# A fused adaLN, state-space convolution and feed-forward kernel: the handover from the convolution's inverse transform to the feed-forward stage rebuilt

## The chip, the cores and the metric

The kernel runs on one core of a Trainium2 chip. A core has TensorE (PE, matrix products into PSUM), VectorE (DVE), ScalarE (ACT), GpSimd (POOL) and SyncE (SP, which issues most of the DMAs here). The metric is the device time of one launch in microseconds. The profile adds the trace of one execution.

## What is computed

The reference, cut to what matters (`_layernorm` has no weights; the sizes are L = 2048 rows, D = 512, N = 128, F = 1792):

```python
def _A_ref(u, ...):                    # a long convolution along L, one kernel for each of D channels
    P = jnp.exp(logdA[:, :, None] * l[None, None, :])
    K = jnp.einsum("dn,dnl,dn->dl", Cc, P, dB).real
    ...                                # y = irfft(rfft(u) * rfft(K)), zero padded to 2 L
    return y + u * Dskip[None, None, :]

def _B_ref(x, w1, b1, w2, b2):
    h = jnp.einsum("bsd,df->bsf", x, w1) + b1
    r = jnp.where(h > zero, h, zero)
    out = jnp.einsum("bsf,fd->bsd", r * r, w2) + b2
    return out

mod = (_silu(c) @ w_mod).reshape(c.shape[0], 6, 1, -1)
sa, ca, ga, sb, cb, gb = ...
h = _layernorm(x) * (1 + ca) + sa
x = x + ga * _A_ref(h, ...)
h = _layernorm(x) * (1 + cb) + sb
x = x + gb * _B_ref(h, ...)
```

## The kernel before

**Stages.** The first 285 us or so normalize the input, make the convolution's kernel for 64 channels at a time (`kgen_*`, eight chunks c = 0 to 7), transform input and kernel in two steps of matmuls (`stage1`, `stage2`), multiply the spectra on VectorE (`product_pieces`, lines 818 to 821) and take the first step of the inverse transform (lines 822 to 838): for each of four groups g of 16 channels, 16 matmuls of 128 columns (real and imaginary part of 64 positions j) go into one PSUM bank, and VectorE copies them (line 834) into `big0` and `big1`, which hold all positions of all chunks. The last chunk, 7, is the last thing of this stage.

**Handover.** `inverse(n)` (line 972) makes four row blocks s = 4n to 4n + 3 of 128 rows. For each s it takes 32 small fp32 matmuls (line 980; 32 by 32 weights `i2c`, 128 moving columns) over four positions of all chunks. Each fp32 matmul leaves two records of a weight load and a matmul in the profile, so one s is 64 records. The sums stand in four PSUM banks: `accs` (two double banks, `tg`) for even n, `tb` (the three `ps` banks and `kg`) for odd n. For n = 0 VectorE adds the input rows (line 989); for the others ScalarE copies (991) and POOL adds (994). `statistics(s)` (998) makes mean and variance on VectorE and a root on ScalarE. `prepare(s)` (1005) normalizes, transposes on TensorE (1021) into a bank of `tb`, and applies the second modulation, scale `cbc` and shift `sbc`, for each quarter q (1024 on VectorE, 1028 on ScalarE); the result h goes to SBUF, is rounded to the matmul's type (1032, `hh`) and the rest is kept apart (1034, `hl`).

**Feed-forward.** Four blocks k of 512 rows, NF = 14 slices t of 128 of F each, i = 14 k + t from 0 to 55. `ffn1(i)` (1076) is 12 matmuls of 512 columns into one bank of `tb` in turn (`tail_bank`): weights high and low against `hh` (1084, 1085), high against `hl` (1087). ScalarE makes relu (1090) and its rounded square (1091), VectorE the exact square (1092) and the rest (1093). `ffn2(i)` (1096) is 12 matmuls into `accs` (1104 to 1106), two steps behind ffn1 (LAG = 2). The rows of the blocks k + 1 are prepared while block k runs.

**What sets the order.** Each engine takes its instructions in a fixed order that `keep_order` (153) writes at build time: a list planner that places groups of instructions by their dependences (`region`, 172, whole banks for PSUM), by durations from `weight` (107) and by the longest path to the end. PE instructions that are in `in_turn` keep their order among themselves.

**Queues.** SyncE issues, in this order around the handover, the input rows (`xt`), the constants `i2c`, the slices of w2 through two staging buffers `wsts` (1043), and the rest of the rows (996). `w2_split` (1039) rounds each slice on ScalarE (929) and subtracts on POOL (930).

Of the kernel before, what the change touches and what calls it, by code (L numbers as in the profile page):

```python
# [11 lines left out]
F32 = mybir.dt.float32  # L12
# [27 lines left out]
HEAD = 4  # L40
ON_DVE = {}
# [65 lines left out]
def weight(ins):  # L107
# [3 lines left out]
    if "DMA" in type(ins).__name__:  # L111
# [10 lines left out]
            if cols == 32 and ins.ins[1].ap[0][1] == 32:  # L122
                return 42, 42 + 130
# [29 lines left out]
def keep_order(tc, traced, slots, in_turn, whole, urgent, behind):  # L153
# [18 lines left out]
    def region(a):  # L172
# [85 lines left out]
    for _ in groups:  # L258
# [7 lines left out]
        if e == "PE":  # L266
# [3 lines left out]
            cost /= level(now)  # L270
# [35 lines left out]
def tile_adaln_ssm_ffn(  # L306
# [61 lines left out]
    tiny = ctile("tiny", [P, 1])  # L368
    rsq = ctile("rsq", [P, 4])
# [80 lines left out]
    pick, second = ctile("pick", [P, 128], FR), ctile("second", [P, 1])  # L450
# [362 lines left out]
    def product_pieces(c):  # L813
        xu, sw, xk = xus[c], sws[c], xks[c]
        yr, yu = spectrum(), spectrum()
        for g in range(4):
# [5 lines left out]
            yield  # L822
        for g in range(4):
            ps = bank("ps", PS)
            for i in range(4):
                for h, y in ((0, yu), (1, yr)):
                    for m in range(2):
                        nc.tensor.matmul(  # L828
                            ps[64 * m : 64 * m + 64, 128 * i : 128 * i + 128],
                            pairs(y)[:, g, i // 2, 64 * m : 64 * m + 64, i % 2],  # L830
                            e1_sb[:, h], start=(h == 0), stop=(h == 1))
            copy = nc.vector.tensor_copy
            for r in range(2):
                copy(z4[r][c][:, :, 4 * g : 4 * g + 4], ps.rearrange("p (d r j) -> p j d r", d=4, r=2)[..., r])  # L834
# [137 lines left out]
    def inverse(n):  # L972
        banks = [t.rearrange("p (i c d) -> p i c d", i=4, c=NC) for t in (accs if n % 2 == 0 else tb)]
        for i in range(4):
            for r in range(2):
                for q in range(4):
                    qs = slice(32 * q, 32 * q + 32)
                    for g in range(4):
                        j = 4 * (4 * n + i) + g
# [3 lines left out]
                        whole[m.ins.name] = f"inverse {n} {i}"  # L983
        if n < 2:
            in_turn.update(whole)
        for q in range(4):
            y = x2[:, 4 * n : 4 * n + 4, q]
            if n == 0:
                nc.vector.tensor_add(y, cd4[:, :, q], banks[q])
            else:  # L990
                nc.scalar.copy(y, banks[q])  # L991
        for s in range(4 * n, 4 * n + 4):
            if n > 0:
# [11 lines left out]
    def prepare(s):  # L1005
        hh, hl = hbuf[s // 4 % 2]
        xn, h32 = (cs_[s], cs_[s]) if s < 4 else cs_[0:2]
        h32 = h32.rearrange("p (q x) -> p q x", q=4)
        if s < 4:
            nc.vector.scalar_tensor_tensor(  # L1010
                mv[:, s, 1:2], mv[:, s, 0:1], -1.0, rstd2[:, s : s + 1], op0=ALU.mult, op1=ALU.mult)
# [10 lines left out]
        for q in range(4):  # L1022
            if s < 4 and q > 0:
                nc.vector.tensor_scalar(
                    h32[:, q, :], tp[:, 128 * q : 128 * q + 128], cbc[:, q : q + 1], sbc[:, q : q + 1],
                    op0=ALU.mult, op1=ALU.add)
            else:
                nc.scalar.activation(
                    h32[:, q, :], tp[:, 128 * q : 128 * q + 128], AF.Identity,
                    bias=sbc[:, q : q + 1], scale=cbc[:, q : q + 1])  # L1030
# [3 lines left out]
        eng.tensor_sub(hl[:, :, 128 * (s % 4) : 128 * (s % 4) + 128], h32, ho.bitcast(F32))  # L1034
# [13 lines left out]
    inverse(0)  # L1048
    inverse(1)
    for s in range(4):  # L1050
        statistics(s)
        prepare(s)
    for i in range(2):
        w2_split(held(kp, f"k0{i}", f"w2{i}", [P, 3072], FR), 3)
    inverse(2)
    inverse(3)
# [11 lines left out]
    r2s = [late_fr[:, 1024:2048], rw[:, 6144:7168], rw[:, 7168:8192]]  # L1068
# [108 lines left out]
```

## Time and profile before

| | us |
|---|---|
| median of 3 runs | 655.47 |
| lowest, highest | 650.13, 662.59 |
| the profiled execution's own time | 654.19 |
| its span | 652.1 |
| TensorE granted clock, mean | 0.976 |

How to read it: a row of the timeline has the start in us, the time covered, the engine, the line, the operation, what is written and read (tiles without their numbers), the shape, how many instructions are merged, and in brackets the idle time of the engine just before and what ended it; "issue" means that the profile shows nothing that the engine waited for. PEld is the weight load. A row of the stages has the length, then for each of PE, PEld, DVE, ACT, POOL the busy time and the number of instructions, then the granted clock of TensorE (1.00 is full), the DMA share and GB/s.

### The profile page before, as it was taken

Reading aid. Unit: us, or ns where it says so; the run is one execution under the profiler, and the core shown is the slowest. Engines: PE = TensorE matmul, PEld = TensorE weight load, DVE = VectorE, ACT = ScalarE, POOL = GpSimd, SP = SyncE. Lnnn points to the kernel's source line nnn. Section 1 sums busy time; section 2 is a strip of 40 time slices with the busy share of each in tenths; the row PEclk is TensorE's granted clock in tenths of the full one; section 3 lists DMA queues with packets and bytes.
Section 4 is the critical chain, followed back from the end, with each engine's and each line's share of the span. In section 5 each row is a group of like instructions: output and inputs, shape, how many; then the busy total and the mean of one; then the engine's idle time right before and its main releaser. Section 6 shows DMA issues by size and latency. Waiting matters only on the chain.

```text
span 652.1 us, 20850 instructions
## 1 busy us (share of the span) xinstructions
PE 594.2 (91%) x9322; PEld 509.1 (78%) x9322; DVE 379.2 (58%) x646; ACT 347.7 (53%) x648; POOL 303.0 (46%) x251
## 2 busy tenths in 40 slices
PE   2389997999999999897769999999999999999995
PEld 2267886999899899885658888888888888888884
DVE  5797778899699789454596532533325332252223
ACT  4957999898997768433745532244322433222220
POOL 5489699999999996078976200011000100000000
PEclk9979999999999999997879999999999999999998
DMA  8932014032022405572141000100001000010001
GB/s 321 376 132 66 4 36 96 8 68 55 17 68 60 124 4 149 137 271 68 55 150 59 2 0 1 64 1 0 2 1 64 1 1 1 0 65 1 0 1 64
DMA packets 21705, 42.30 MB, mean 65 GB/s; under 512 B 3696, under 2 KB 9200, under 8 KB 20336
## 3 DMA queue, kind: packets, MB, share of 16 engines
q1 hardware_dynamic: 21184, 40.84, 20.3%
q8 instruction: 73, 1.20, 0.8%
q10 hardware_dynamic: 432, 0.14, 0.1%
q14 instruction: 16, 0.13, 0.1%
HBM read 28.39 MB, written 4.19 MB: 50 GB/s over the span
## 4 chain that ended last, share of the span: by engine, by line
PE 77%; ACT 6%; DVE 5%; POOL 4%; issue 4%; DMA 3%; SPq 0%; DVEq 0%; POOLq 0%; ACTq 0%
PE tg L1104 8%; PE tg L1105 8%; PE tg L1106 8%; PE ps L671 7%; PE ps L681 7%; PE ps L828 7%; PE ps L1085 6%; PE ps L1084 6%; PE ps L1087 6%; PE kg L809 4%; PE ps L634 3%; PE kg L1085 2%; PE kg L1084 2%; PE kg L1087 2%; ACT tables L756 1%
## 5 line engine op out<-in xcount | busy, mean ns | idle before, releaser
L1092 DVE TENSOR_TENSOR xy<-xy 128x512 f32<-128x512 f32 x56 | 45.8, 818 | 163.1 <-ACT rw L1091 106.4
L1090 ACT ACTIVATE xy<-ps,b1c 128x512 f32<-128x512 f32 x42 | 28.9, 689 | 134.5 <-PE ps L1087 134.5
L1017 POOL TENSOR_TENSOR big<-big,lo 128x512 f32<-128x512 f32 x12 | 16.0, 1332 | 158.5 <-DVE xy L1014 158.5
L681 PE MATMUL ps<-xy,t_sb 128*64 128x64 f32 x2048 | 66.7, 223 | 5.6 <-issue 3.3
L681 PEld LDWEIGHTS ps<-xy,t_sb 128*64 128x64 f32 x2048 | 63.5, 138 | 7.9 <-issue 3.6
L828 PE MATMUL ps<-e_sb,xy 128*64 128x128 f32 x1024 | 62.0, 274 | 2.8 <-issue 2.3
L828 PEld LDWEIGHTS ps<-e_sb,xy 128*64 128x64 f32 x1024 | 56.6, 138 | 4.7 <-issue 3.2
L673 ACT COPY xy<-ps 128x512 f32<-128x512 f32 x64 | 37.1, 591 | 15.3 <-PE ps L671 14.9
L789 POOL TENSOR_TENSOR rtl<-tables 128x1024 f32<-128x1024 f32 x22 | 43.4, 1971 | 0.2
L819 DVE TENSOR_TENSOR xy<-ps,xy 128x512 f32<-128x512 f32 x64 | 39.8, 680 | 2.0 <-PE ps L681 1.6
L1084 PE MATMUL ps<-h0h,w1h 128*128 128x512 f32 x88 | 35.3, 401 | 0.5 <-ACT big L991 0.5
L834 DVE COPY big<-ps 128x256 f32<-128x256 f32 x64 | 24.1, 417 | 19.8 <-PE ps L828 19.8
L765 POOL TENSOR_TENSOR llph<-lo,big 128x1024 int32<-128x1024 int32 x16 | 34.7, 2169 | 0.7 <-ACT tg L777 0.7
L765 POOL TENSOR_TENSOR rtl<-lo,big 128x1024 int32<-128x1024 int32 x16 | 34.3, 2142 | 1.5 <-ACT tg L777 1.0
L671 PE MATMUL ps<-d_sb,ksb 128*64 128x128 f32 x512 | 33.9, 275 | 1.1 <-DVE xy L819 0.8
L1090 ACT ACTIVATE xy<-kg,b1c 128x512 f32<-128x512 f32 x14 | 9.7, 690 | 47.1 <-PE kg L1087 42.8
L671 PE MATMUL ps<-d_sb,big 128*64 128x128 f32 x512 | 31.6, 274 | 0.8 <-ACT big L637 0.7
L1084 PE MATMUL ps<-h,w1h 128*128 128x512 f32 x80 | 31.6, 395 | 0.0
L1093 DVE TENSOR_TENSOR rw<-xy,rw 128x512 fp32r<-128x512 f32 x37 | 28.6, 774 | 2.9
L671 PEld LDWEIGHTS ps<-d_sb,ksb 128*64 128x64 f32 x512 | 28.1, 137 | 2.5 <-DVE xy L819 1.0
L671 PEld LDWEIGHTS ps<-d_sb,big 128*64 128x64 f32 x512 | 28.4, 137 | 1.6 <-ACT big L637 1.0
L800 DVE TENSOR_TENSOR rtl<-rtl,tg 128x1024 f32<-128x1024 f32 x22 | 26.7, 1213 | 2.4 <-POOL rtl L789 2.4
(260 smaller groups left out, 1604.0 us busy)
## 6 DMA issues: line engine op xcount, KB each, us to landing
xy<-xt SPq DMA_DIRECT2D x32, 256.0 KB, 4.4
xy<-xy SPq DMA_DIRECT2D x16, 512.0 KB, 6.2
xy<-w_mod SPq DMA_DIRECT2D x6, 1024.0 KB, 8.4
out_dram<-xy SPq DMA_DIRECT2D x16, 256.0 KB, 2.1
xy<-w SPq DMA_DIRECT2D x14, 256.0 KB, 3.1
raw<-w SPq DMA_DIRECT2D x6, 512.0 KB, 6.3
t_sb<-c_t SPq DMA_DIRECT2D x1, 2048.0 KB, 11.6
i2c<-c_i SPq DMA_DIRECT2D x1, 2048.0 KB, 8.5
```

The costliest lines, as they stand in the source:

```text
L671: nc.tensor.matmul(ps[64 * r : 64 * r + 64, 128 * i : 128 * i + 128], src[:, i], d1_sb[:, r], start=True, stop=True)
L681: nc.tensor.matmul(ps[64 * r : 64 * r + 64, 64 * i : 64 * i + 64].rearrange("p (h q t) -> p q h t", h=2, t=2), t2_sb[:, 8 * g + i, r], src ...
L765: nc.gpsimd.tensor_tensor(ph.rearrange("p d r (a b) -> p (d r) a b", a=4), bc(low_phase[:, us].rearrange("p d r b -> p (d r) b"), 2, 4), b ...
L789: nc.gpsimd.tensor_mul(am[:, 0, :, 32:96].rearrange("p d (v x) -> p d v x", v=2), bc(et[:, 256 + 8 * d0 : 384 + 8 * d0].rearrange("p (y a) ...
L828: nc.tensor.matmul(ps[64 * m : 64 * m + 64, 128 * i : 128 * i + 128], pairs(y)[:, g, i // 2, 64 * m : 64 * m + 64, i % 2], e1_sb[:, h], st ...
L1084: pe.append(nc.tensor.matmul(ps, w1h[:, q, fs], hh[:, q, :], start=(q == 0), stop=False))
L1085: pe.append(nc.tensor.matmul(ps, wl[:, q], hh[:, q, :], start=False, stop=False))
L1087: pe.append(nc.tensor.matmul(ps, w1h[:, q, fs], hl[:, q, :], start=False, stop=(q == 3)))
L1092: nc.vector.tensor_mul(rr, rr, rr)
L1104: pe.append(nc.tensor.matmul(acc, r2l[:, ms], hi_, start=(t == 0), stop=False))
L1105: pe.append(nc.tensor.matmul(acc, r2h[:, ms], lo_, start=False, stop=False))
L1106: pe.append(nc.tensor.matmul(acc, r2h[:, ms], hi_, start=False, stop=(t == NF - 1)))
```

## The change

It touches the last chunk's inverse sums, the row blocks 0 to 15 on their way to the feed-forward stage, and the squares.

- *Sums by position.* For chunk 7 alone, `product_pieces` first sums the positions j = 0 to 15 of all 16 channels (64 matmuls of 32 columns, one bank), copies them, and then sums the other 48 positions, group by group (64 matmuls of 96 columns, four banks).
- *Inverse in twos.* `inverse(s0, n)` takes s0 and a count: 0 and 1, then 2 and 3, both in the first halves of the same four `accs` areas, then fours from 4 (in `tb`), 8 and 12 (in `accs`).
- *Scale and shift in PSUM.* The modulation writes back into the transposes' bank, a whole bank by one engine (VectorE for s = 0 and 2, ScalarE for all others); rounding and subtraction read that bank, and the subtraction is VectorE's for every s.
- *Squares in PSUM.* The exact square is now (h + b1) times relu, one operation that reads and writes the product's bank; the subtraction reads it there.
- *Half blocks.* The first two products of the feed-forward stage are made in two halves of 256 columns each; the product of step 3 is made before the first `ffn2`.
- *Rest.* Three small constants share a tile; the two early w2 tiles are longer by 512 and hold a part of r2; in the planner a 32 by 32 matmul counts 24 instead of 42 ns with a floor of 0.75 for its clock, and a `tg` tile counts as one region.

```diff
             if cols == 32 and ins.ins[1].ap[0][1] == 32:
-                return 42, 42 + 130
+                return 24, 24 + 130
...
-        if t.name[:2] in ("ps", "tg", "kg"):
+        if t.name[:2] == "tg":
+            return t.name, 15, 1
+        if t.name[:2] in ("ps", "kg"):
...
-    tiny = ctile("tiny", [P, 1])
-    rsq = ctile("rsq", [P, 4])
+    small = ctile("small", [P, 8])
+    tiny, rsq, second = small[:, 0:1], small[:, 1:5], small[:, 5:6]
...
+        def sums(ps, g, i, js):
+            for h, y in ((0, yu), (1, yr)):
+                for m in range(2):
+                    nc.tensor.matmul(
+                        ps[64 * m : 64 * m + 64], pairs(y)[:, g, i // 2, 64 * m : 64 * m + 64, i % 2],
+                        e1_sb[:, h].rearrange("p (r j) -> p r j", r=2)[:, :, js], start=(h == 0), stop=(h == 1))
...
+        j0 = 0
+        if c == NC - 1:
+            j0 = 16
+            ps = bank("ps", PS).rearrange("p (d r j) -> p d r j", d=16, r=2)
+            for d in range(16):
+                sums(ps[:, d], d // 4, d % 4, slice(0, j0))
+            spread(ps, slice(0, j0), slice(0, 16))
...
-    def inverse(n):
-        banks = [t.rearrange("p (i c d) -> p i c d", i=4, c=NC) for t in (accs if n % 2 == 0 else tb)]
+    def inverse(s0, n):
+        banks = [t.rearrange("p (i c d) -> p i c d", i=4, c=NC)[:, 0:n] for t in (tb if s0 == 4 else accs)]
...
         for q in range(4):
-            if s < 4 and q > 0:
+            part = tp[:, 128 * q : 128 * q + 128]
+            if s in (0, 2):
                 nc.vector.tensor_scalar(
-                    h32[:, q, :], tp[:, 128 * q : 128 * q + 128], cbc[:, q : q + 1], sbc[:, q : q + 1],
-                    op0=ALU.mult, op1=ALU.add)
+                    part, part, cbc[:, q : q + 1], sbc[:, q : q + 1], op0=ALU.mult, op1=ALU.add)
...
+        h32 = tp.rearrange("p (q x) -> p q x", q=4)
...
-        eng = nc.gpsimd if s < 4 else nc.vector
-        eng.tensor_sub(hl[:, :, 128 * (s % 4) : 128 * (s % 4) + 128], h32, ho.bitcast(F32))
+        nc.vector.tensor_sub(hl[:, :, 128 * (s % 4) : 128 * (s % 4) + 128], h32, ho.bitcast(F32))
...
-    inverse(0)
-    inverse(1)
+    inverse(0, 2)
+    inverse(2, 2)
...
-    inverse(2)
-    inverse(3)
+    for s in (4, 8, 12):
+        inverse(s, 4)
...
+    EARLY = 2
+    early = [tail_bank() for _ in range(EARLY)]
+    for i in range(EARLY):
+        ffn1_products(i, early[i], slice(0, 256))
...
-        nc.vector.tensor_mul(rr, rr, rr)
-        nc.vector.tensor_sub(r2l, rr, r2h.bitcast(F32))
+        nc.vector.scalar_tensor_tensor(ps, ps, b1c[:, t : t + 1], rr, op0=ALU.add, op1=ALU.mult)
+        nc.vector.tensor_sub(r2l, ps, r2h.bitcast(F32))
...
         if i < 4 * NF:
-            ffn1(i)
+            if i not in held_banks:
+                ffn1(i)
+            square(i)
+        if i == LAG:
+            ffn1(i + 1)
```

The order of the engines changes from chunk 7's sums on. On TensorE, before, the last group's sums (the `e_sb` rows; `xy` holds the products, `ps` the bank) run straight into the inverse (`i2c` rows, `tg` the banks):

```order
L828 MATMUL ps_161<-e_sb,xy_95 64x128 x2
L828 MATMUL ps_161<-e_sb,xy_93 64x128 x2
L980 MATMUL tg_427<-big_84,i2c 32x128 x8
L980 MATMUL tg_428<-big_84,i2c 32x128 x8
L980 MATMUL tg_427<-big_85,i2c 32x128 x8
L980 MATMUL tg_428<-big_85,i2c 32x128 x8
```

Now, at the same place, the second pair of row blocks (the first four rows are its last one), the transposes (`ident`) of block 0, the last group's sums, and the transposes of block 1 ahead of the inverse of block 8:

```order
L997 MATMUL tg_425<-big_83,i2c 32x128 x8
L997 MATMUL tg_426<-big_83,i2c 32x128 x8
L997 MATMUL tg_425<-big_84,i2c 32x128 x8
L997 MATMUL tg_426<-big_84,i2c 32x128 x8
L1037 MATMUL ps_158<-ident,xy_91 128x128 x4
L830 MATMUL ps_157<-e_sb,xy_94 64x96 x2
L830 MATMUL ps_157<-e_sb,xy_92 64x96 x2
...
L1037 MATMUL ps_159<-ident,xy_91 128x128 x4
L997 MATMUL tg_425<-big_83,i2c 32x128 x8
```

The last sums moved from ahead of the whole inverse to behind its first four row blocks.

Later on TensorE, before, three products of the feed-forward stage (`h0l` ends each) stand ahead of the first second product (`tg` from `w1lc`, which holds the rest of the square):

```order
L1087 MATMUL ps_160<-h0l,w1h 128x512 x4
...
L1087 MATMUL ps_161<-h0l,w1h 128x512 x4
...
L1087 MATMUL kg_364<-h0l,w1h 128x512 x4
L1104 MATMUL tg_427<-w_5020,w1lc 128x512
L1105 MATMUL tg_427<-w_5020,w1lc 128x512
```

Now the inverse of row block 13 is followed by the four half products, a whole one, row block 14, another whole one, row block 15, and the first second product:

```order
L997 MATMUL tg_426<-big_84,i2c 32x128 x8
L1102 MATMUL ps_158<-h0h,w1h 128x256
...
L1105 MATMUL ps_158<-h0l,w1h 128x256 x4
...
L1105 MATMUL ps_159<-h0l,w1h 128x256 x4
...
L1105 MATMUL kg_362<-h0l,w1h 128x512 x4
...
L1105 MATMUL ps_157<-h0l,w1h 128x512 x4
...
L1136 MATMUL tg_425<-w_4948,w1lc 128x512
```

Two row blocks of the inverse moved behind the first products, and a fourth product ahead of the first second one.

On VectorE, before, the first squares stand behind the statistics of the row blocks (`st`, `mv`, `rstd`):

```order
L1000 BN_STATS st_74<-big_84 128x6
L1003 RECIPROCAL rstd_77<-rstd_77 128x1
L1001 BN_AGGR mv_72<-st_74 128x2
L1092 TENSOR_TENSOR xy_96<-xy_96 128x512
L1093 TENSOR_TENSOR w1lc<-xy_96,w1lc 128x512
```

Now the normalization of row block 4 (`xy_91` from `big_83`) is just ahead of them, and the squares are in the products' banks:

```order
L1030 TENSOR_SCALAR xy_91<-big_83,mv_71,rstd_76 128x512
L1018 BN_AGGR mv_71<-st_73 128x2
L1124 SCALAR_TENSOR_TENSOR ps_158<-ps_158,b1c,xy_95 128x512
L1125 TENSOR_TENSOR w1lc<-ps_158,w1lc 128x512
L1020 RECIPROCAL rstd_76<-rstd_76 128x1
```

The squares moved ahead of most of the statistics, and their first input from SBUF to PSUM.

More of the change, by code (lines that the diff above doesn't have):

```diff
@@ L269, in keep_order @@
             shape = kind
-            cost /= level(now)
+            cost /= max(level(now), 0.75 if kind == 32 and groups[g][0].ins[1].ap[0][1] == 32 else 0)
             a = now
@@ L822, in product_pieces, with spread @@
             yield
+        def sums(ps, g, i, js):
[4 more added lines that the diff above has]
+                        e1_sb[:, h].rearrange("p (r j) -> p r j", r=2)[:, :, js], start=(h == 0), stop=(h == 1))
+        def spread(ps, js, ds):
+            for r in range(2):
+                nc.vector.tensor_copy(z4[r][c][:, js, ds], ps.rearrange("p d r j -> p j d r")[..., r])
+        j0 = 0
[5 more added lines that the diff above has]
+            spread(ps, slice(0, j0), slice(0, 16))
+            yield
         for g in range(4):
-            ps = bank("ps", PS)
+            ps = bank("ps", PS).rearrange("p (d x) -> p d x", d=4)[:, :, 0 : 128 - 2 * j0]
+            ps = ps.rearrange("p d (r j) -> p d r j", r=2)
             for i in range(4):
[L826 to L834, printed above, removed]
+                sums(ps[:, i], g, i, slice(j0, 64))
+            spread(ps, slice(j0, 64), slice(4 * g, 4 * g + 4))
             if g == 3:
@@ L970, in tile_adaln_ssm_ffn @@
     whole, in_turn = {}, set()
[L972 to L974 removed]
+    def inverse(s0, n):
+        banks = [t.rearrange("p (i c d) -> p i c d", i=4, c=NC)[:, 0:n] for t in (tb if s0 == 4 else accs)]
+        for i in range(n):
             for r in range(2):
```

58 lines of the change are left out of this document (33 added, 25 removed).

## The prediction, made before the changed kernel was run

> **What bounds the kernel now.** I read the page first, then the busy time of each engine by stage, then the timeline of the stage that stood out. The page's totals say TensorE; the stages say where it is not busy.
>
> ```profile
> span 652.1 us, 20850 instructions
> 290.00:320.00 30.00, 22.75 (x1005) 18.47 (x1005) 17.40 (x44) 15.16 (x31) 26.04 (x20) 0.78 0.27 84
> 320.00:340.00 20.00, 13.17 (x161) 10.23 (x132) 13.71 (x19) 9.34 (x20) 16.70 (x14) 0.84 0.44 132
> 420.00:500.00 80.00, 80.00 (x358) 65.60 (x358) 30.11 (x47) 27.06 (x49) 5.17 (x4) 1.00 0.05 19
> ```
>
> From 340 us on TensorE (first column after the length) has no gap, so the end moves one for one with the moment at which that stretch begins. The handover, 290 to 340, is the only late stage with idle TensorE: 14.1 of 50 us, at a granted clock of 0.78 and 0.84. Its marks in the timeline:
>
> ```profile
> 285.84 7.21 PE L828 MATMUL ps<-e_sb,xy 128*64 128x128 f32 x128
> 293.62 1.46 PE L980 MATMUL tg<-big,i2c 32*32 32x128 f32 x94 [0.57 <-issue]
> 295.66 1.93 PE L980 MATMUL tg<-big,i2c 32*32 32x128 f32 x128 [0.58 <-issue]
> 299.13 0.72 PE L980 MATMUL tg<-big,i2c 32*32 32x128 f32 x34 [1.54 <-issue]
> 302.88 0.42 PE L980 MATMUL kg<-big,i2c 32*32 32x128 f32 x1 [1.33 <-issue]
> 306.61 0.42 PE L980 MATMUL kg<-big,i2c 32*32 32x128 f32 x1 [0.89 <-issue]
> 317.10 0.42 PE L980 MATMUL ps<-big,i2c 32*32 32x128 f32 x12 [1.91 <-DVE xy L1024]
> 321.59 0.33 PE L980 MATMUL ps<-big,i2c 32*32 32x128 f32 x7 [0.60 <-issue]
> 323.10 0.50 PE L1084 MATMUL ps<-h0h,w1h 128*128 128x512 f32 x1 [0.54 <-ACT big L991]
> q8 instruction: 73, 1.20, 0.8%
> PE 594.2 (91%) x9322; PEld 509.1 (78%) x9322; DVE 379.2 (58%) x646; ACT 347.7 (53%) x648; POOL 303.0 (46%) x251
> ```
>
> Call 285.84 M0 (last chunk's sums, L828) and 323.10 M1 (first FFN product). Inside the inverse (L980) TensorE stops with nothing to wait for ("issue"), after 128 records: restarts at 295.66, 299.13, 302.88 and 306.61 lie 3.47, 3.75 and 3.73 apart, mean 3.65, though 128 records take 1.93. The queue row fits: 1.20 MB in 73 packets is 16.4 KB each, and TensorE's 2 x 9322 records over 73 are 255 per packet, 128 matmuls with their loads. I read that as a supply of instructions of at most 128 records in 3.65 us; slower rows (128 of L828 in 7.21) never meet it.
>
> The Trainium skill ("Runtime: NRT & Kernel Launch", Instruction fetch mechanics) has instructions refilled in blocks of 256 and calls the cost of a block's boundary "mostly hidden". The block size agrees with the 255; hidden it is not in the inverse. With it hidden, the sum below would be the rival's 644.
>
> After M1 comes the other wait:
>
> ```profile
> 329.81 3.77 POOL L994 TENSOR_TENSOR big<-big,xy 128x512 f32<-128x512 f32 x3
> 329.87 6.69 DVE L1092 TENSOR_TENSOR xy<-xy 128x512 f32<-128x512 f32 x1 [0.33 <-ACT w1lc L1091]
> 333.49 1.30 POOL L930 TENSOR_TENSOR rw<-xy,rw 128x512 fp32r<-128x512 f32 x1
> 334.71 1.30 POOL L994 TENSOR_TENSOR big<-big,xy 128x512 f32<-128x512 f32 x1
> 337.34 0.79 PE L1104 MATMUL tg<-w,w1lc 128*128 128x512 f32 x1 [5.69 <-DVE w1lc L1093]
> 338.00:340.00 2.00, 2.00 (x6) 1.58 (x5) 1.89 (x3) 1.72 (x4) 0.69 (x1) 0.50 0.00 0
> 341.97 0.39 PE L1084 MATMUL ps<-h0h,w1h 128*128 128x512 f32 x1
> 344.72 0.40 PE L1104 MATMUL tg<-w,rw 128*128 128x512 f32 x1
> 347.49 0.60 PE L1021 MATMUL ps<-ident,xy 128*128 128x128 f32 x4
> 347.85 0.48 PE L1084 MATMUL ps<-h0h,w1h 128*128 128x512 f32 x1
> L1092 DVE TENSOR_TENSOR xy<-xy 128x512 f32<-128x512 f32 x56 | 45.8, 818 | 163.1 <-ACT rw L1091 106.4
> ```
>
> VectorE's square, 0.69 us elsewhere, took 6.69: it ended when POOL's five operations did (336.01). So the first second product (L1104) came 5.69 us late, and then ran at half clock: 12 matmuls in 4.63 (337.34 to 341.97) against 2.77 (344.72 to 347.49). M2 = 347.85 is the product of FFN step 4, and behind it nothing changes: M2 carries the whole result.
>
> **The change, part by part.** It is costed against the profiled execution: 654.19 us, span 652.1, 1.28 below the median shown (655.47). Up to M0 all five engines keep their order, and SyncE keeps its order throughout. The packed constants, the longer w2 tiles and the other places of r2 add no instruction: nothing. The planner's numbers act only through the order.
>
> ```profile
> 277.86 3.90 PE L681 MATMUL ps<-xy,t_sb 128*64 128x64 f32 x128
> 284.86 0.76 DVE L834 COPY big<-ps 128x256 f32<-128x256 f32 x2 [0.98 <-PE ps L828]
> 299.73 2.48 DVE L989 TENSOR_TENSOR big<-xy,tg 128x512 f32<-128x512 f32 x4 [5.88 <-PE tg L980]
> 314.96 1.04 DVE L1024 TENSOR_SCALAR xy<-kg,cbc,sbc 128x128 f32<-128x128 f32 x3
> 348.19 1.51 ACT L1028 ACTIVATE xy<-ps,sbc,cbc 128x128 f32<-128x128 f32 x4 [1.22 <-PE ps L1021]
> 318.00 2.03 ACT L991 COPY big<-tg 128x512 f32<-128x512 f32 x4
> 315.93 5.15 POOL L1034 TENSOR_TENSOR h0l<-xy,h0h 128x512 fp32r<-128x512 f32 x4
> L1000 DVE BATCH_NORM_STATS2 st<-big 128x6 f32<-128x512 f32 x12 | 8.1, 677 | 5.4 <-POOL big L994 5.3
> L819 DVE TENSOR_TENSOR xy<-ps,xy 128x512 f32<-128x512 f32 x64 | 39.8, 680 | 2.0 <-PE ps L681 1.6
> L1010 DVE SCALAR_TENSOR_TENSOR mv<-mv,rstd 128x1 f32<-128x1 f32 x4 | 2.8, 697 | 0.1
> 312.69 0.42 PEld L1021 LDWEIGHTS ps<-ident,xy 128*128 128x128 f32 x4 [0.66 <-ACT big L991]
> ```
>
> *Sums by position.* 64 matmuls of 128 columns become 64 of 32 and 64 of 96. For 32 columns no row stands: by columns 7.21/4 = 1.8, by the same weights with 64 columns (L681) 3.90. I take 3.7, near L681, whose loads never pause. 96 columns: 7.21 x 3/4 = 5.4. TensorE pays 9.1 for 7.2, two copies (about 0.8) come on VectorE, and records rise by 128.
>
> *Inverse in twos, M0 to M1.* I walk the chain with 0.1 to 0.2 us per hop. First positions summed by 289.6 and copied by 290.5; inverse 0 and 1 behind a block's edge end at 293.7. Four half adds (2.48/2 in all), statistics (0.68 each), the small product (697 ns today, beside POOL; taken as 0.2, an estimate, since its second tensor input goes; at 0.7 the walk is up to 2 later) and ScalarE's normalization follow, with sums and copies between. The copies of the last 96-column bank stand on VectorE behind the second pair's adds and statistics: done near 303.9, against 293.9 now. Inverse 8 waits there; that wait is new. Scale, shift, rounding and subtraction follow in PSUM; the fourth subtraction on VectorE ends near 312.6 and only then are the banks of inverse 4 to 7 free (today this edge is L1024's at 317). Then 384 records, one block waiting and two at 3.65: 1.93 + 7.3 = 9.2. M1 comes at 321.8, 36.0 after M0 instead of 37.26: **1.3 gained**. Bounds: the records from M0 to M1 are as many as before (128 + 1024 + 16 = 1168; now 256 + 896 + 16, as inverses 14 and 15 come after M1), so at full supply 1168/128 x 3.65 = 33.3; the other end is today's 37.3 with the 1.9 of the sums, 39.2.
>
> *Scale and shift in PSUM.* No row writes PSUM from ScalarE or VectorE. Bounds: as fast as into SBUF (L1028 0.38, L1024 0.35 in a row) or, as each now waits for the one before it in its bank, twice that; on the path lie four of ScalarE's and four of VectorE's, so 0 to 2.9. I take 0.1 each, from what a hop costs. POOL loses 5.15, VectorE gains 4 x 0.68; had POOL kept them they would not end the chain.
>
> *Half blocks, M1 to M2.* In the order all four half products stand together behind the last rounding and behind inverse 13, so they start nothing earlier. 48 matmuls of 256 columns: at least the load's 0.42/4 = 0.105, at most 0.19 as loads show beside 512 columns; near the first, 0.12: 5.8 for 5.54. Then two products (2 x 2.77), inverse 14 and 15 (1.93, at a place where the supply keeps up), the copies of their banks by ScalarE, of which two must be done (2.03/2), with hops and the statistics queued ahead of them 1.6 of waiting, two second products (5.54) and transposes (0.36): 20.8 instead of 24.75, **3.95 gained**. It holds one FFN product more before the second product, so squares and subtractions have time.
>
> *Square in PSUM.* The product now reads one input from PSUM. The nearest row, L819 (680 ns in the stretch where POOL is busiest), shows no lockout, so the 6.69 goes; what is late next are ScalarE's copies of inverse 15 and the statistics of VectorE ahead of them. Ends: 0.68, or 6.69 again.
>
> Sum: 1.3 + 3.95 = 5.25, 654.19 - 5.25 = **648.9**; say 649 (650 from the median). Best ends: 33.3 and 19.2 (no wait) make 9.5, 644.7. Worst: 39.2, and 20.8 + 3.4 (loads at 0.19) + 1.86 (half clock again) + 3 (wait as long as 4.6) = 29.1 make 6.3 lost, 660.5.
>
> **Rivals.**
>
> ```profile
> L1014 DVE TENSOR_SCALAR xy<-big,mv,rstd x12: 532/546/1523, 318.5 to 529.3; 128x512 f32<-128x512 f32 x12
> 500.00:600.00 100.00, 100.00 (x443) 81.59 (x443) 33.34 (x51) 32.11 (x56) 3.87 (x3) 1.00 0.04 16
> 345.64 0.63 ACT L1091 ACTIVATE w1lc<-xy 128x512 fp32r<-128x512 f32 x1
> ```
>
> *Supply hidden.* If sums between the inverses let blocks arrive in time, my walk without block waits reaches M1 at 317.0: 6.1 + 3.95, about **644**. For it: no pause at L828 or in the FFN. Against it: four pauses in a row in L980, and the record count is unchanged.
>
> *The lockout moves.* On VectorE the normalization of row block 4 (L1014, now L1030) stands just ahead of the first square, SBUF to SBUF, and takes 1523 at worst against 532. Its turn comes near 321.7, when POOL has six operations of 1.3 queued, up to one that waits for it. Held until 329.1, VectorE's list (nine operations of 0.7 and the small ones, 9.0 in all) ends at 338.7; ScalarE's copies start behind it, the second product at 340.3, cold: M2 = 340.3 + 4.63 + 2.77 + 0.36 = 348.1, **654.5**, no gain. It decides once L1030 ends after 327. Against: L1014's first, at 318.5, ran under POOL's four L1034 (315.93 to 321.08), and the worst of all twelve is 1523 ns.
>
> The Trainium skill ("SBUF — State Buffer", Who interferes with whom) has VectorE blocked by POOL with two SBUF inputs or in a two-port mode, which tensor_scalar can enter, not with one SBUF input. L1092's 6.69 and L819's 680 agree; by it L1030 can block too, which gives this rival's 654.5.
>
> *Banks held longer (the other side).* A product's bank is now free after relu, square, product and subtraction (0.63 to 0.7 each, as L1091 and L819, with hops 3 us) instead of after relu; the transposes' bank likewise. If the FFN must wait, it does so in 56 steps: 0.1 us each eats the 5.25, 0.35 makes 19.6 - 5.25 = 14.4 lost, **668.6**. Against: a bank returns after four others, two steps of 5.5 at the least, and VectorE is 33% busy. It decides where VectorE is some 6 us late.
>
> **How the numbers follow.** The sum 0.52 (own range 645 to 653), supply hidden 0.22, lockout 0.18, banks 0.04, 0.04 for what I don't see. Three runs spread from 650.13 to 662.59, so about 2% (13 us) is what a measurement tells from no change. Faster by that needs the hidden supply and a warm start with the runs' scatter: 0.10. Slower: the banks and half the unseen, 0.05. Same 0.85. From 641 (hidden supply with scatter) to 657 (lockout with scatter) lie 8 in 10.
>
> **What would show it.** Right: restarts in the inverse still 3.5 to 3.8 apart; first FFN product 35 to 37 after the sums start; squares near 0.7; step 4's product some 57 after the start of the sums instead of 62.0. Wrong: gaps at "issue" gone (hidden supply); L1030 over 5 us (lockout); TensorE waiting for VectorE inside 420 to 600 (banks); half products at 0.19.

## The result and the profile after

| | before | after |
|---|---|---|
| median, us | 651.57 (20 runs, 646.89 to 662.59) | 648.27 (20 runs, 643.95 to 651.57) |
| ratio, 95% interval | | 0.9947 (0.9926 to 0.9968) |
| profiled execution's own time; span | 654.19; 652.1 | 646.79; 645.0 |

The change makes the kernel about 3.4 us faster (0.53% of 651.57): the interval lies clear of 1, but the gain is below the 2% under which two times count as the same here. The ratios leave out executions more than 1.5% above the fastest of the same kernel: of the kernel before, none of 17 where it is compared with d1, u1, u3 and v1 (labels of the table below), 3 of 29 with c1, c2, v2 and the changed kernel once more, and 12 of 29 with a1, p1, p2 and v3. The forecast of 649 lies 0.7 us from the median. Its reasons do not fare as well, as the runs below show.

The page and the timeline of TensorE of the kernel after give M0 (the start of the last chunk's sums, L830 now), the restarts inside the inverse (L997), M1 (the first product of the feed-forward stage, L1102), the first second product (L1136) and M2 (the product of step 4):

```profile
span 645.0 us, 21178 instructions
286.50 5.38 PE L830 MATMUL ps<-e_sb,xy 128*64 128x32 f32 x160
313.15 0.46 PE L997 MATMUL ps<-big,i2c 32*32 32x128 f32 x6 [0.58 <-issue]
316.89 0.46 PE L997 MATMUL ps<-big,i2c 32*32 32x128 f32 x6 [0.89 <-issue]
320.89 1.42 PE L997 MATMUL tg<-big,i2c 32*32 32x128 f32 x52 [1.11 <-issue]
322.25 0.58 PE L1102 MATMUL ps<-h0h,w1h 128*128 128x256 f32 x1
338.42 0.50 PE L1136 MATMUL tg<-w,w1lc 128*128 128x512 f32 x1 [1.03 <-ACT big L1008]
344.37 0.48 PE L1102 MATMUL ps<-h0h,w1h 128*128 128x512 f32 x1
```

M0 to M1 is 322.25 - 286.50 = 35.75 us, M1 to M2 is 22.12, together 57.87 instead of 62.01. From M2 to the end it is 645.0 - 344.37 = 300.63, and before it was 652.1 - 347.85 = 304.25. So this pair of profiles has 4.14 us of gain in the handover and 3.62 behind it, where the prediction had none; M0 itself came 0.66 later. Together 7.10, the difference of the spans, and about twice what the medians differ by. So at least one of the two is partly an accident of one execution, and the experiments were made to find which.

The stages of the kernel after, read as before (length; busy time and count for PE, PEld, DVE, ACT, POOL; the granted clock third from the end):

```profile
312.00:326.00 14.00, 11.41 (x345) 9.06 (x336) 2.43 (x6) 4.74 (x10) 8.14 (x7) 0.52 0.30 90
500.00:600.00 100.00, 100.00 (x450) 82.79 (x449) 35.11 (x52) 33.04 (x56) 3.89 (x3) 1.00 0.03 11
```

In the second row TensorE has no gap, before and after, at a clock of 1.00, yet it runs 450 matmuls in 100 us instead of 443. The first row shows a half clock in the middle of the handover.

### The profile page after: what moved, and what is told of

Read it like the earlier page. It is cut to its first block, busy times and chain, and to the rows that moved or that the text cites. A ratio compares the mean times of both kernels' runs of the same rounds, so it can differ in the third digit from the quotient of the medians.

```text
span 645.0 us, 21178 instructions
## 1 busy us (share of the span) xinstructions
PE 593.0 (92%) x9474; PEld 511.8 (79%) x9474; DVE 370.1 (57%) x652; ACT 351.2 (54%) x652; POOL 297.0 (46%) x247
## 3 DMA queue, kind: packets, MB, share of 16 engines
q1 hardware_dynamic: 21184, 40.84, 20.8%
## 4 chain that ended last, share of the span: by engine, by line
PE 79%; ACT 8%; DVE 5%; issue 4%; DMA 1%; POOL 1%; DVEq 0%; ACTq 0%
PE tg L1136 8%; PE tg L1137 8%; PE tg L1138 8%; PE ps L830 7%; PE ps L674 7%; PE ps L684 7%; PE ps L1102 6%; PE ps L1103 6%; PE ps L1105 6%; PE kg L812 3%; PE ps L637 3%; PE kg L1102 2%; PE kg L1103 2%; PE kg L1105 2%; ACT tables L759 2%
## 5 line engine op out<-in xcount | busy, mean ns | idle before, releaser
L1124 DVE SCALAR_TENSOR_TENSOR ps<-ps,b1c,xy 128x512 f32<-128x512 f32 x42 | 31.8, 757 | 113.8 <-ACT xy L1122 113.7
L684 PE MATMUL ps<-xy,t_sb 128*64 128x64 f32 x2048 | 68.1, 225 | 5.5 <-issue 3.2
L684 PEld LDWEIGHTS ps<-xy,t_sb 128*64 128x64 f32 x2048 | 64.8, 140 | 8.0 <-issue 3.7
L830 PE MATMUL ps<-e_sb,xy 128*64 128x128 f32 (+2 forms) x1152 | 64.1, 265 | 2.5 <-issue 2.0
L830 PEld LDWEIGHTS ps<-e_sb,xy 128*64 128x64 f32 x1152 | 58.8, 139 | 4.4 <-issue 2.8
L1102 PE MATMUL ps<-h0h,w1h 128*128 128x512 f32 (+1 forms) x96 | 36.9, 388 | 0.0
L836 DVE COPY big<-ps 128x256 f32<-128x256 f32 (+1 forms) x66 | 24.2, 407 | 17.1 <-PE ps L830 17.1
L1102 PE MATMUL ps<-h,w1h 128*128 128x512 f32 x80 | 31.4, 393 | 0.0
L1124 DVE SCALAR_TENSOR_TENSOR kg<-kg,b1c,xy 128x512 f32<-128x512 f32 x14 | 10.6, 755 | 34.0 <-ACT xy L1122 34.0
```

Source lines behind the costliest of these rows:

```text
L684: nc.tensor.matmul(ps[64 * r : 64 * r + 64, 64 * i : 64 * i + 64].rearrange("p (h q t) -> p q h t", h=2, t=2), t2_sb[:, 8 * g + i, r], src ...
L830: nc.tensor.matmul(ps[64 * m : 64 * m + 64], pairs(y)[:, g, i // 2, 64 * m : 64 * m + 64, i % 2], e1_sb[:, h].rearrange("p (r j) -> p r j" ...
L1102: pe.append(nc.tensor.matmul(ps, w1h[:, q, fs], hh[:, q, cols], start=(q == 0), stop=False))
L1124: nc.vector.scalar_tensor_tensor(ps, ps, b1c[:, t : t + 1], rr, op0=ALU.add, op1=ALU.mult)
```

## Experiments

All marks in one table, each from the TensorE timeline of that kernel's profile (us; the last two columns are the span minus M2 and the ratio of times to the kernel before with its interval). The first six rows have the work in the order of the kernel before. In d1 and c2 the planner also put some statistics, copies and slices of w2 into other places, and so it did in u1 against the changed kernel; these three test the edit with its new order.

| kernel | M0 | M0 to M1 | M1 to M2 | M0 to M2 | M2 to end | ratio |
|---|---|---|---|---|---|---|
| before | 285.84 | 37.26 | 24.75 | 62.01 | 304.25 | |
| before + square in PSUM (d1) | 285.46 | 38.13 | 19.94 | 58.07 | 304.27 | 0.9896 (0.9857 to 0.9934) |
| before + packed constants (c1) | 284.17 | 37.41 | 20.41 | 57.82 | 300.61 | 0.9940 (0.9910 to 0.9970) |
| before + places of r2 (c2) | 287.29 | 39.84 | 19.13 | 58.97 | 304.34 | 0.9991 (0.9957 to 1.0024) |
| before, tiles 64 bytes up (p1) | 286.44 | 38.63 | 21.28 | 59.91 | 305.45 | 1.0009 (0.9969 to 1.0049) |
| before, tiles 32 bytes up (p2) | 287.79 | 36.89 | 21.01 | 57.90 | 305.41 | 1.0000 (0.9958 to 1.0043) |
| after | 286.50 | 35.75 | 22.12 | 57.87 | 300.63 | 0.9947 (0.9926 to 0.9968) |
| after, once more | 284.74 | 39.25 | 22.11 | 61.36 | 300.60 | 0.9938 (0.9908 to 0.9968) |
| after, constants unpacked (a1) | 286.94 | 37.11 | 23.04 | 60.15 | 304.31 | 1.0024 (0.9987 to 1.0062) |
| after, square in SBUF (u1) | 287.92 | 37.14 | 21.81 | 58.95 | 300.63 | 0.9938 (0.9906 to 0.9971) |
| after, sums whole (u3) | 289.14 | 35.14 | 21.57 | 56.71 | 300.65 | 0.9884 (0.9831 to 0.9937) |
| after, inverse beside products (v1) | 289.16 | 25.26 | 30.31 | 55.57 | 300.67 | 0.9816 (0.9773 to 0.9858) |
| v1, sums whole (v2) | 288.65 | 24.22 | 27.72 | 51.94 | 300.61 | 0.9841 (0.9794 to 0.9889) |
| v2, no half blocks (v3) | 289.17 | 24.25 | 29.70 | 53.95 | 300.68 | 0.9845 (0.9795 to 0.9895) |

### One part alone, one part undone, and another order

**Square in PSUM alone.**

```diff
-        nc.vector.tensor_mul(rr, rr, rr)
-        nc.vector.tensor_sub(r2l, rr, r2h.bitcast(F32))
+        nc.vector.scalar_tensor_tensor(ps, ps, b1c[:, t : t + 1], rr, op0=ALU.add, op1=ALU.mult)
+        nc.vector.tensor_sub(r2l, ps, r2h.bitcast(F32))
```

> The kernel before with the square in PSUM and nothing else of the change. My theory: POOL's lock on the square (6.69 us) goes, the first second product (L1104) no longer waits 5.69, and it starts warm, 2.77 instead of 4.63. The stretch from the first to step 4's product (M1 to M2) falls from 24.75 to about 17.2, M0 to M1 stays at 37.3, the time falls by some 7.5 us (ratio 0.988 to the kernel before), which is more than the whole change gave (0.9947). Rival: something stands right behind the lock (the statistics that wait for POOL's additions, or the banks held longer), then M1 to M2 is 21 or more and the ratio 0.995 or above. The lock stays (other rival): L1092 near 6 us, ratio 1.00.

VectorE's and POOL's rows of this kernel (start, length, engine, line, operation, shapes):

```profile
329.84 0.76 DVE L1092 SCALAR_TENSOR_TENSOR ps<-ps,b1c,xy 128x512 f32<-128x512 f32 x1
330.08 5.12 POOL L994 TENSOR_TENSOR big<-big,xy 128x512 f32<-128x512 f32 x4
```

The lock is gone: with POOL at work the square takes 0.76. TensorE does not wait for the first second product at all. But M1 to M2 is 19.94, not 17.2: the first products ran at half clock here (0.50 from 324 to 328), while in the kernel before those products ran at full pace and the first second product was the slow one. The ratio is as expected (0.988 expected, 0.9896 measured), and this part alone is at least as good as the whole change. Its profile is 4.3 us shorter than that of the kernel before, its median 7.0 (655.15 to 648.18); where the rest lies the profiles do not show.

**The changed kernel with the square in SBUF.** The same four lines, the other way round.

> The changed kernel with only its square back in SBUF (two SBUF inputs). My theory: the lock returns: one of the first squares takes over 3 us while POOL adds rows, the first second product waits 3 to 6 us longer than the 1.03 of the changed kernel, M1 to M2 grows from 22.1 to 25 to 28, and the ratio to the kernel before is 1.000 to 1.005. Rival: in the changed order the squares have slack enough, M1 to M2 stays within 1 of 22.1 and the ratio near 0.995.

The theory fell. VectorE's first square, the subtraction behind it, and POOL's row around them:

```profile
332.17 0.73 DVE L1124 TENSOR_TENSOR xy<-xy 128x512 f32<-128x512 f32 x1 [4.65 <-ACT w1lc L1123]
332.94 1.69 DVE L1125 TENSOR_TENSOR w1lc<-xy,w1lc 128x512 fp32r<-128x512 f32 x1
328.53 5.55 POOL L1011 TENSOR_TENSOR big<-big,xy 128x512 f32<-128x512 f32 x4
```

The square of two SBUF inputs took 0.73 beside POOL, which lost time instead (5.55 for four additions, 5.00 to 5.12 elsewhere). Behind it both paid a little: the subtraction took 1.69 instead of 0.69, and the second square, at 334.55, 1.77. So interference is still there, but nothing as long as 6.69. In the changed order the square's place does not matter, 21.81 against 22.12. The Trainium skill ("SBUF — State Buffer", Who interferes with whom) says that the order of issue, not the shape of the operation, decides who blocks. These rows agree: the same operation took 6.69 in one order and 0.73 in another, in which POOL lost the time.

**The changed kernel with whole sums.** In `product_pieces` the branch for the last chunk is never taken:

```diff
-        if c == NC - 1:
+        if False:
             j0 = 16
```

> The changed kernel with the last chunk's sums made whole, as before (64 matmuls of 128 columns), and no sums by position. My theory: supply of instructions and not the start of the inverse sets M1, so the early start buys nothing: M0 to M1 is 33 to 36 against 35.75, with 128 fewer records on the way, and the ratio to the kernel before is 0.990 to 0.995. Rival, the purpose of that step: without it the first pair starts some 3.5 us later and M1 with it, M0 to M1 38 or more, ratio 0.997 or above.

As the theory had it: M0 to M1 is 35.14, so the start of the inverse 3 us earlier buys nothing. The ratio 0.9884, a little better than expected, is below that of the changed kernel, though the intervals still overlap.

**The inverse beside the products.** One expression in `inverse`:

```diff
-        banks = [t.rearrange("p (i c d) -> p i c d", i=4, c=NC)[:, 0:n] for t in (tb if s0 == 4 else accs)]
+        banks = [t.rearrange("p (i c d) -> p i c d", i=4, c=NC)[:, 0:n] for t in accs]
```

Blocks 4 to 7 no longer need the banks in which h stands, so the planner starts the products as soon as h is there and puts row blocks 8 to 15 among them.

> The changed kernel with one word changed: all row blocks of the inverse use the accs banks, so that the tail banks are free and the first products need not stand behind the inverse of blocks 4 to 13; 8 of the 12 later row blocks then stand among the first products. My theory (records are supplied at 128 per 3.7 us): a product's matmuls take 0.23 us each, so the supply runs ahead there and the inverse costs its own 1 us per row block: M0 to M1 falls from 35.75 to 26 to 29, M1 to M2 grows to 24 to 28, M2 comes 51 to 56 after M0 instead of 57.9, ratio to the kernel before 0.985 to 0.992. Rival: the copies of the accs banks by ScalarE and POOL's additions are late instead; TensorE then waits for ACT at L997 or L1136 by what it gained, and the ratio stays 0.994 or above.

M1 comes 25.26 after M0. M1 to M2 is longer than expected (30.31; it has a 1.47 us stop at "issue" inside the fifteenth of the sixteen row blocks, and a half clock from 332 to 335), but M2 still comes 55.57 after M0, and the kernel is 1.84% faster than before, more than expected. The rival fell: the wait for ScalarE at L1136 is 1.03, as it was.

### What lies behind M2

The stretch from M2 to the end was 304.25 and 304.27 in two kernels and 300.63 to 300.67 in four, far too exact for scatter. What differs is the pace of matmuls that read certain tiles, w1lc among them. These are the first of 12 matmuls of a second product, and the first matmul behind them, of before and then of after:

```profile
508.80 0.39 PE L1104 MATMUL tg<-w,w1lc 128*128 128x512 f32 x1
511.60 0.40 PE L1084 MATMUL kg<-h0h,w1h 128*128 128x512 f32 x1
```

```profile
503.43 0.39 PE L1136 MATMUL tg<-w,w1lc 128*128 128x512 f32 x1
506.15 0.39 PE L1102 MATMUL kg<-h0h,w1h 128*128 128x512 f32 x1
```

2.80 us for twelve before, 2.72 after, with no wait in either. The kernel before has the better pace too, where both operands lie in tiles that the change leaves in place (`rw`; w1h with the second half buffer h1, here h):

```profile
468.86 1.07 PE L1087 MATMUL ps<-h,w1h 128*128 128x512 f32 x4
469.77 0.39 PE L1104 MATMUL tg<-rw 128*128 128x512 f32 x1
472.49 0.39 PE L1084 MATMUL kg<-h,w1h 128*128 128x512 f32 x1
507.87 1.09 PE L1087 MATMUL ps<-h0l,w1h 128*128 128x512 f32 x4
```

Twelve matmuls out of `rw` take 2.72 there. It isn't a matter of weights alone: four matmuls with the weights w1h take 0.91 on h1 (468.86 to 469.77) and 0.93 on h0l (507.87 to 508.80), and of these three tiles only h0l is moved. Two of the change's parts move tiles, both of which the prediction had put at nothing.

**Packed constants alone; places of r2 alone.** The first is

```diff
-    tiny = ctile("tiny", [P, 1])
-    rsq = ctile("rsq", [P, 4])
+    small = ctile("small", [P, 8])
+    tiny, rsq, second = small[:, 0:1], small[:, 1:5], small[:, 5:6]
...
-    pick, second = ctile("pick", [P, 128], FR), ctile("second", [P, 1])
+    pick = ctile("pick", [P, 128], FR)
```

By the program's allocation each of the three constants had 32 bytes of a partition of SBUF to itself; in one tile they have 32 together, so all tiles allocated behind them on that side (`lo`, `big0`, h0h, h0l, w1la to w1lc, w2d) lie 64 bytes lower. The second edit is

```diff
-        w2_split(held(kp, f"k0{i}", f"w2{i}", [P, 3072], FR), 3)
+        w2_split(early_w2[i], 3)
...
-    r2s = [late_fr[:, 1024:2048], rw[:, 6144:7168], rw[:, 7168:8192]]
+    r2s = [halves(late_fr[:, 1024:2048]), tuple(t[:, 3072:3584] for t in early_w2), halves(rw[:, 6144:7168])]
```

with `early_w2` two tiles of 3584 columns, as in the change.

> The kernel before with only the three small constants packed into one tile; every tile behind them on that side of SBUF lies 64 bytes lower, and the order of the work is that of before. In the profiles so far the stretch from step 4's product (M2) to the end was 304.25 and 304.26 us where the constants lay apart, and 300.63, 300.63, 300.65 and 300.67 where they were packed and the r2 tiles had their new places. Theory P: the packing is the cause. M2 to the end falls to about 300.6, the second products whose r2 lies in the w1lc tile take 2.72 instead of 2.80, the handover stays at 62, and the ratio to the kernel before is about 0.9945. Theory R: the places of r2 are the cause; M2 to the end stays at 304.2, ratio 1.000.

> The kernel before with only the other places of r2 (the second of its three places at the ends of the two longer early w2 tiles). Theory R: M2 to the end falls to about 300.6, ratio about 0.9945. Theory P: it stays at 304.2 and the ratio between 0.998 and 1.002. If each did half, both kernels would show some 302.4.

Theory P holds. The stages of c1 and then of c2:

```profile
500.00:600.00 100.00, 100.00 (x449) 82.75 (x448) 33.42 (x50) 30.81 (x52) 3.03 (x3) 1.00 0.03 11
```

```profile
500.00:600.00 100.00, 100.00 (x444) 81.63 (x443) 33.82 (x51) 32.31 (x56) 3.90 (x3) 1.00 0.03 11
```

The 64 bytes alone raise the 443 matmuls in 100 us to 449 and cut M2 to the end from 304.25 to 300.61; the places of r2 do nothing (444 and 304.34). The ratio of c1, 0.9940, is that of the whole change.

But c1's handover is not 62, as was expected of it: 57.82, in the order of the kernel before, with the square still in SBUF. Its VectorE, POOL and TensorE rows:

```profile
328.14 3.45 DVE L1092 TENSOR_TENSOR xy<-xy 128x512 f32<-128x512 f32 x1 [1.19 <-ACT w1lc L1091]
327.23 3.81 POOL L994 TENSOR_TENSOR big<-big,xy 128x512 f32<-128x512 f32 x3
331.45 1.28 POOL L930 TENSOR_TENSOR rw<-xy,rw 128x512 fp32r<-128x512 f32 x1 [0.42 <-ACT rw L929]
333.33 0.50 PE L1104 MATMUL tg<-w,w1lc 128*128 128x512 f32 x1 [1.14 <-DVE w1lc L1093]
341.99 0.48 PE L1084 MATMUL ps<-h0h,w1h 128*128 128x512 f32 x1
```

The square is locked out here too, until POOL pauses for a slice that ScalarE has not yet rounded (0.42 at 331.45). That pause came early enough to leave TensorE a wait of 1.14, where the profile on which the prediction rests had 5.69. The two shifted kernels below have the same order again: waits of 1.27 and 1.37. So the 5.69 is one execution of four; c2, with its few differences of order, has no wait there at all.

**The changed kernel once more.**

> The changed kernel once more, beside the others on the same chip. If the handover's gain (4.1 us) and the faster tail (3.6) are its own, M2 comes 57 to 58.5 after M0, M2 to the end is 300.6 again, and the ratio lies between 0.988 and 0.994. If one of them was the scatter of one profile, M2 to the end comes out near 304 or the handover near 62.

The tail is 300.60 again; the handover is 61.36. Of its M0 to M1 (39.25 instead of 35.75) the largest piece is one stop:

```profile
293.75 1.54 PE L997 MATMUL tg<-big,i2c 32*32 32x128 f32 x66 [2.64 <-issue]
```

The second of the expectation's cases has come: the tail (M2 to the end) is the change's own, the 4.1 us of the handover were one profile against another.

**The changed kernel with the constants unpacked.** The c1 edit backwards.

> The changed kernel with its three small constants in tiles of their own again, so that the tiles behind them lie where they lay before, 64 bytes higher. If the whole measured gain of the change was the packing's (M2 to the end 300.6 instead of 304.3) and the rebuilt handover nets nothing, M2 to the end is 304.3 and the ratio to the kernel before 0.997 to 1.003. Rival: the rebuilt handover has a gain of its own, 2 to 4 us; then the ratio is 0.994 to 0.997.

```profile
500.00:600.00 100.00, 100.00 (x444) 81.64 (x443) 34.78 (x51) 33.04 (x56) 3.86 (x3) 1.00 0.04 14
```

The tail is slow again (304.31, 444 matmuls) and no gain is left that the ratio shows: 1.0024 (0.9987 to 1.0062). By the medians of all executions, 652.77 and 654.52, it is 0.9973. So no gain of the rebuilt handover as a whole is shown, but one of some 2 us isn't excluded.

**Tiles 64 and 32 bytes higher.** In the kernel before, `ctile("tiny", [P, 24])[:, 0:1]` and `[P, 16]` in place of `[P, 1]`.

> The kernel before with one small constant's tile longer, so that the tiles behind it lie 64 bytes higher than before (those of the changed kernel lie 64 lower); the order of the work is that of before. If the place within 128 bytes decides (32 before, 96 in the changed kernel and here, 96 also for the tiles of the other side), M2 to the end is 300.6 and the ratio near 0.994. If only lower is faster, or the place within 256 bytes decides (224 in the changed kernel, 96 here), it stays at 304.3 or above and the ratio near 1.000.

> The kernel before with those tiles 32 bytes higher: their starts lie at 64 within 128 bytes, on a whole multiple of 64, which neither kernel has had. If a start on a multiple of 64 is what weight loads want, M2 to the end is 300.6 or less. If the two sides' having the same place within 128 bytes is what counts (96 on the other side), it stays near 304.3.

Both are slower behind M2, 305.45 and 305.41, by 1.2 us. The place within 128 bytes does not decide, nor does a start on a multiple of 64. Of the four places tried, one is good (300.6) and three are not. By the allocation the good one puts these tiles 480 bytes past a multiple of 512, where the tiles of the other side (`rw`, w1h) lie too; the others are at 32, 64 and 96. Whether 512 is the period, and whether the other side's place matters, was not tried. With the tiles 32 bytes up, the four matmuls of w1h on h1 take 0.93 as well (467.09 to 468.02), though neither operand moved, so what meets what in SBUF stays open.

**The best orders together.** v2 has both edits of u3 and v1; v3 is v2 with `EARLY = 0`.

> The changed kernel with both: all row blocks of the inverse in the accs banks (so that the first products stand among row blocks 8 to 15) and the last chunk's sums whole. Alone, the first brought M2 to 55.6 after M0 instead of 57.9, the second to 56.7. If they add, M2 comes 54.0 to 55.0 after M0 and the ratio to the kernel before is 0.977 to 0.985. Rival: each takes the same slack of the supply of instructions, M2 stays at 55.6 or later and the ratio at that of the first alone, 0.982 or above.

> The best kernel so far (inverse beside the products, sums whole; M2 51.9 after M0, ratio 0.984) with its first two products whole, not in half blocks. My theory: half blocks cost 5.8 for 5.54 at most and start nothing earlier, so without them M2 comes 51 to 52.5 after M0 and the ratio is 0.980 to 0.987. Rival, their purpose: the first products wait for all four row blocks and the last of them is then late: M0 to M1 grows by 1 or more and M2 with it, to 53 or more.

Marks and stages of v2:

```profile
288.65 7.21 PE L830 MATMUL ps<-e_sb,xy 128*64 128x128 f32 x128
312.87 0.38 PE L1102 MATMUL ps<-h0h,w1h 128*128 128x256 f32 x1
315.93 1.91 PE L997 MATMUL tg<-big,i2c 32*32 32x128 f32 x128
326.21 2.17 PE L997 MATMUL tg<-big,i2c 32*32 32x128 f32 x143
328.72 0.94 PE L997 MATMUL tg<-big,i2c 32*32 32x128 f32 x49 [0.34 <-issue]
334.64 0.50 PE L1136 MATMUL tg<-w,w1lc 128*128 128x512 f32 x1 [1.03 <-ACT big L1008]
340.59 0.48 PE L1102 MATMUL ps<-h0h,w1h 128*128 128x512 f32 x1
312.00:326.00 14.00, 14.00 (x386) 11.71 (x375) 8.84 (x20) 10.12 (x22) 9.29 (x9) 1.00 0.41 117
```

M2 comes 51.94 after M0, earlier than both gains together would give (and than the 54 to 55 expected). Between 312 and 326 us TensorE has no gap and the full clock, where the changed kernel had 0.52. The time, 642.17 us, stands beside 648.41 for the changed kernel on the same chip and 652.28 for the one before. v1, v2 and v3 can't be told apart by their intervals; all three beat both kernels.

v3 shows the half blocks to start nothing: M0 to M1 is 24.25 with whole products, 24.22 with halves. M2 comes 53.95 after M0, later than the 51 to 52.5 expected: the stretch behind M1 is 2 us longer in the profile and holds one stop of 1.95 at "issue" and a half clock from 330 to 333.5. The ratios, 0.9845 and 0.9841, show no difference.

## Why the prediction was right

The number was right by luck: three errors nearly cancel. The 5.25 us of the handover do not show in the profiles; 3.6 came in a part that was costed at nothing; and the sum started from an execution of 654.19, 2.6 above the median of the kernel before (651.57). 654.19 - 2.6 - 3.6 = 648.0 is close to the measured 648.27, and so is 654.19 - 5.25 = 648.9. By its steps:

**"Behind it nothing changes: M2 carries the whole result."** This is the step that failed. That TensorE has no gap behind M2 says that no wait can be gained there, not that its matmuls have the pace they could have. The failed entry of the sum is "the packed constants ... add no instruction: nothing": c1 has 3.64 us from it (304.25 - 300.61), a1 loses 3.7 without it, and by the ratios it is the whole measured change (0.9940 alone, 0.9947 and 0.9938 for all).

**The handover, 5.25 gained.** Also failed, in what it was measured against. The term was worked out against one profile with a handover of 62.01. Three more profiles in the same order (c1, p1, p2) have 57.82, 59.91 and 57.90; with the first their mean is 59.4. The rebuilt handover has 57.87, 61.36 and 60.15, mean 59.8. The profile was an unlucky one, and the 5.69 us wait and the half clock behind it (1.86), some 7.5 us in all, were priced as if each execution paid them. The mean of the waits of all four is (5.69 + 1.14 + 1.27 + 1.37) / 4 = 2.4.

**M0 to M1, 36.0.** It came as 35.75 in the first profile, then 39.25 and 37.11: mean 37.4. The four of the order before have 37.26, 37.41, 38.63 and 36.89, mean 37.5. The 1.3 of gain isn't there.

**Supply of instructions.** Held, and seen directly. Cut into windows of 0.25 us, the trace has the instruction queue move one packet in the windows that start at 306.50, 310.50, 314.25, 318.25 and 322.00, 3.75 to 4.0 apart. In these 15.5 us TensorE restarts at 313.15, 316.89 and 320.89, 3.74 and 4.00 apart, each 2.64 or 2.65 behind the start of such a window. The Trainium skill ("Runtime: NRT & Kernel Launch", Instruction fetch mechanics) has the next block fetched while the current one runs. That agrees with v2, where matmuls of 0.12 to 0.23 us stand between those of the inverse and TensorE has no gap from 312 to 326 us; in the inverse by itself a block lasts 1.93, about half of the time between restarts. The rival "supply hidden" thus fell for this change, and came about in v2.

**Sums by position, 1.9 paid for an early start.** The start earns nothing: M0 to M1 is 35.14 without it (u3), and 35.75, 39.25 and 37.11 with it. The price was nearer 2.6: the changed kernel's three rows of these sums (from 286.50, 293.81 and 300.65 on) take 5.38, 2.86 and 1.54, together 9.78, against 7.21 before.

**Scale and shift in PSUM, 0.1 more each.** Right. VectorE's and ScalarE's rows of the changed kernel:

```profile
305.47 1.77 DVE L1041 TENSOR_SCALAR kg<-kg,cbc,sbc 128x128 f32<-128x128 f32 x4
307.29 1.84 ACT L1044 ACTIVATE ps<-ps,sbc,cbc 128x128 f32<-128x128 f32 x4
```

0.44 and 0.46 in a row, against 0.35 and 0.38 into SBUF. The prediction's "No row writes PSUM from ScalarE or VectorE" is a misreading: L777, on ScalarE, writes 1024 columns of `tg` in 1.13, a row that could have narrowed the bounds.

**Half blocks, 5.8.** Mis-sized: 7.28 (322.25 to 329.53). At full clock a half matmul takes 0.12, as taken; the first 15 or so ran at half clock at 0.21, which the sum did not have since it put the stretch at half clock with the wait that goes. In the profiles of the kernels that run the whole inverse up to row block 13 ahead of the products, 14 to 24 us between M0 and M2 have the half clock. It moves about (mainly 300 to 310 and 334 to 341 in the profile before, 312 to 325 in the one after) and did not go with the wait that was removed; in v1 to v3, with fewer stops, it is 7 to 10 us.

**M1 to M2, 20.8.** It came as 22.12, 22.11 and 23.04, against 20.41, 21.28 and 21.01 before where the lock was short. The two row blocks and the wait for ScalarE (1.03; 1.6 predicted) that now stand there cost about what the shorter wait saves.

**Square in PSUM.** Right in mechanism (0.76; alone 0.9896), but the rebuilt order has no use for it (u1). From d1 to a1 the ratio goes from 0.9896 to 1.0024 (0.9894 to 0.9973 by the medians of all executions), so the rest of the rebuild gives back much or all of what this line gains. How that return divides among position sums, twos and half blocks isn't shown, and why d1 gains 7.0 us when its handover of 58.07 is only 1.3 below the mean of the order before isn't either; in the profiles a1 has 3.10 more than d1 from M1 to M2 and 1.02 less from M0 to M1. The kernel before with this line and the packed constants together was not run.

**The other rivals.** The moved lockout fell, since L1030 takes 0.70:

```profile
323.66 0.70 DVE L1030 TENSOR_SCALAR xy<-big,mv,rstd 128x512 f32<-128x512 f32 x1
```

Banks held longer fell too: TensorE has no gap in the stretch from 500 to 600 us, and M2 to the end did not grow, even with the constants unpacked (304.31 against 304.25).

## What to carry to other kernels

A gap-free engine is not an engine at its best pace: count its instructions per 100 us in the stretch of the profile that is said to be full, and cost each edit that moves tiles in memory, even by 64 bytes, as a change with two signs. A wait that hangs on how two queues happen to meet (here the lock) or on the supply of instructions must not be priced from one profile; take the stretch between two marks in several executions first. And where small matmuls outrun their instructions, put long ones between them: moving the inverse among the products (v1, 0.9816) gave more than starting it earlier did (the changed kernel, 0.9947).

## What the runs showed of the hardware that was not expected

- Tiles that TensorE reads 64 bytes lower in SBUF: 12 matmuls of 512 columns in 2.72 us instead of 2.80, at the same granted clock of 1.00 and without a wait. 32 or 64 bytes higher costs about 1.2 us over the last 305 instead.
- A VectorE operation with two SBUF inputs beside a busy POOL took 6.69, 3.45, 1.77 or 0.73 us, which went with when it met POOL's queue.
- M0, ahead of which the kernels hardly differ, lay between 284.17 and 289.17 in the fourteen profiles. TensorE's stops at "issue" ahead of it vary; why the kernels with the latest M0 (u3 and v1 to v3, 288.65 to 289.17) agree so well stays open.
